# A linear attention block with a squared-ReLU MLP: w_in's products of four slices in pairs by seven block products

## The chip, the cores and the metric

One core of a Trainium2 chip runs the whole program. The metric is device time in microseconds, from the first to the last instruction; the number for a kernel is the median over its runs.

## The reference

Linear attention with a decay per head, in blocks along the sequence (4 batches, 8 heads, 768 positions, 64 features a head), and then an MLP over the 3072 tokens:

```
intra = ((q_block @ k_block.T) * decay_mask) @ v_block
inter = (q_block * lam**(pos+1)) @ kv_state
out   = intra + inter
kv_state = lam**block * kv_state + (k_block * lam**(block-1-pos)).T @ v_block

x = out, laid out as (3072, 512)
h = x @ w_in            # w_in  (512, 2048)
g = max(h, 0)**2
result = g @ w_out      # w_out (2048, 512)
```

All inputs and the result are float32.

## The kernel before

Tokens are taken in tiles of C = 128, NT = 24 of them (six to a batch), t counting them; G = 4 tiles make a slice of N = 512 tokens, and there are NM = 6 slices, m = 0 to 5 (in the text, slice 1 is m = 0). The 2048 hidden features are NF = 16 blocks of 128, f counting them.

A float32 product is made of three products of reduced float32 (F32R): each operand is split into a high part and the rest, and high x high, rest x high and high x rest are added. The weights lie split in SBUF for the whole program, `wh` and `wl`, w_in's block f in place `w_in(f)` and w_out's in `w_out(f)`; the loading, rounding and splitting of the weights is spread over slice 1.

One step (m, f) is `hidden(m, f)`, twelve matmuls of 512 columns into a PSUM bank `h` (4 pieces of the 512 inner features x 3 parts), then on ScalarE `square(h)` (ReLU, square rounded to `gh`, square), on VectorE `rest` (the difference `gl`), and `project`, twelve matmuls of 512 columns that add to the slice's four output banks `acc`. `project` of a step stands in the next step, behind the next `hidden`, so that ScalarE and VectorE have twelve matmuls of time. After f = 15 the four banks are copied out and stored.

The attention of a slice is made during the slice before it: in the steps f of slice m tile t = 4(m+1) + f // 4 is taken, in four parts by f % 4: `prep_k` and, behind the projection, `scores` (part 0), `prep_q` and `masked` (1), `attend` (2: the update of the state, the products within the block and with the state, and `split`, which makes `xh` and `xl` of the result), `decay` (3). So half a tile's matmuls at most stand between two products of w_in. `attend` is followed by the loads of tile t + 2 (`load_qk`, `load_kv`), into two buffers taken in turn. `prep_q`, `prep_k` and `decay` run on GpSimd, all transfers are issued by SP.

The order on every engine is the order in which the code is written; nothing reorders it. Waits are semaphores between the engines, put in where data or buffers need them. PSUM has four `acc` banks, two `h` banks and two for attention (`ps_a`: first the two score banks, then the banks of the output o and of the state update u).

Of the kernel before, what the change touches and what calls it, by code (L numbers as in the profile page):

```python
# [19 lines left out]
NCB = S // C  # L20
NT = B * NCB
DM = H * D
DF = 2048
KT = DM // P
NF = DF // P
G = 4
N = G * C
NM = NT // G

NLOT = NF + 1


@with_exitstack
def body(ctx: ExitStack, tc: tile.TileContext, qT, kT, kvq, lam, w, out):
    nc = tc.nc
    const = ctx.enter_context(tc.tile_pool(name="const", bufs=1))
    io = ctx.enter_context(tc.tile_pool(name="io", bufs=2))
    wk = ctx.enter_context(tc.tile_pool(name="wk", bufs=2))  # L40
    small = ctx.enter_context(tc.tile_pool(name="small", bufs=1))
    ps_acc = ctx.enter_context(tc.tile_pool(name="ps_acc", bufs=G, space=PSUM))
    ps_h = ctx.enter_context(tc.tile_pool(name="ps_h", bufs=2, space=PSUM))
    ps_a = ctx.enter_context(tc.tile_pool(name="ps_a", bufs=2, space=PSUM))
    V = nc.vector
# [12 lines left out]
    kv = const.tile([P, NPR, P], F32, name="kv")  # L58
# [9 lines left out]


    feat, tok, lent = {}, {}, {}  # L70

    def load_qk(t):
        if t in (2, 3):
            lent[t] = wk.tile([P, 2, KT * C, 2], F32, name=f"lent{t}", tag=("xh", "xl")[t - 2])
            x = lent[t][:, 0].rearrange("p a b -> p (a b)")
        else:
            x = io.tile([P, 2 * DM], F32, name="qk_sb")
        feat[t] = x.rearrange("p (k a b) -> p k a b", k=2, a=NPR)
        for k, y in enumerate((kT, qT)):
            nc.sync.dma_start(out=feat[t][:, k], in_=y[t])  # L80

    def load_kv(t):
        if t in (2, 3):
            x = lent[t][:, 1].rearrange("p a b -> p (a b)")
        else:
            x = io.tile([P, 2 * DM], F32, name="kv_sb")
        nc.sync.dma_start(out=x, in_=kvq[t, :, 0 : 2 * DM])
        x = x.rearrange("p (k h d) -> p k h d", k=2, h=H)
        tok[t] = x[:, 0], x[:, 1]


    wh = const.tile([P, 2 * NF, DM], F32R, name="wh")
    wl = const.tile([P, 2 * NF, DM], F32R, name="wl")

    def w_in(f):
        return 2 * f - 1 if f else 0

    def w_out(f):
        return 2 * f + 2 if f < NF - 1 else 2 * NF - 1
# [29 lines left out]
    def first(u):  # L129
        first_hi(u)  # L130
        first_lo(u)
# [167 lines left out]
    def scores(t, pool, name):  # L299
        sc_of[t] = [pool.tile([P, DM], F32, name=name) for _ in range(2)]  # L300
        k_, q_ = feat[t][:, 0], feat[t][:, 1]
        for p in range(NPR):
            for j, r in enumerate(rows):
                nc.tensor.matmul(  # L304
                    sc_of[t][j][:, p * C : (p + 1) * C], k_[r, p], q_[r, p],
                    start=True, stop=True, skip_group_check=True,
                )

    def prep_q(t):
        if t % NCB:  # L310
            nc.gpsimd.tensor_tensor(out=feat[t][:, 1], in0=feat[t][:, 1], in1=qpow, op=ALU.mult)  # L311

    def prep_k(t):
        if t % NCB < NCB - 1:
            x = tok[t][0].rearrange("p (a j) d -> p a j d", j=2)
            y = near.rearrange("p j a c -> p a j c")[:, :, :, T - 1 : T]
            nc.gpsimd.tensor_tensor(out=x, in0=x, in1=y.broadcast_to([P, NPR, 2, D]), op=ALU.mult)

    def masked(t):
        a_of[t] = []  # L320
        for j in range(2):
            a = wk.tile([P, NPR, C], F32, name="a", tag="gl" if t in (1, 3) else "a")
            V.tensor_tensor(  # L323
                out=a, in0=sc_of[t][j].rearrange("p (a b) -> p a b", a=NPR),
                in1=mask[:, j], op=ALU.mult,
            )
            a_of[t].append(a)
# [38 lines left out]
    def split(t, o):  # L366
        xh, xl = xs_of[t // G]
        cs = slice(t % G * C, (t % G + 1) * C)
        o = o.rearrange("p (a b) -> p a b", a=KT)
        nc.scalar.copy(xh[:, :, cs], o)  # L370
        return lambda: V.tensor_tensor(
            out=xl[:, :, cs], in0=o, in1=xh[:, :, cs].bitcast(F32), op=ALU.subtract
        )

    def attend(t):

        o = ps_a.tile([P, DM], F32, name="att")
        u = ps_a.tile([P, DM], F32, name="att")
        news(t, u)
        within(t, o, True, not t % NCB)  # L380
        before(t, o, False, True)
        update(t, u)
        split(t, o)()

    def decay(t):
        if t % NCB < NCB - 2:
            for j, r in enumerate(rows):
                nc.gpsimd.tensor_tensor(  # L388
                    out=kvd[r], in0=kv[r, :, rows[j]],
                    in1=qpow[r, :, C - 1 : C].broadcast_to([D, NPR, D]), op=ALU.mult,  # L390
                )


    g_of, accs, stage = {}, {}, []

    def hidden(m, f, xh, xl):
        h = ps_h.tile([P, N], F32, name="h")
# [9 lines left out]
    def square(h):  # L407
        nc.scalar.activation(h, h, AF.Relu)  # L408
        gh = wk.tile([P, N], F32R, name="gh")
        nc.scalar.activation(gh, h, AF.Square)  # L410
        nc.scalar.activation(h, h, AF.Square)  # L411
        return gh

    def rest(m, f, r, gh):
        gl = wk.tile([P, N], F32R, name="gl")
        V.tensor_tensor(out=gl, in0=r, in1=gh.bitcast(F32), op=ALU.subtract)  # L416
        g_of[m, f] = gh, gl

    def project(m, f):
        gh, gl = g_of.pop((m, f))  # L420
        if f == 0:
            accs[m] = [ps_acc.tile([P, DM], F32, name="acc") for _ in range(G)]
        end = f == NF - 1
        j = w_out(f)

        def high(i):
            cs = slice(i * C, (i + 1) * C)
            nc.tensor.matmul(accs[m][i], gh[:, cs], wh[:, j], start=f == 0, stop=False)  # L428
            nc.tensor.matmul(accs[m][i], gh[:, cs], wl[:, j], start=False, stop=False)  # L429

        def low(i):
            cs = slice(i * C, (i + 1) * C)
            nc.tensor.matmul(accs[m][i], gl[:, cs], wh[:, j], start=False, stop=end)  # L433
            if end:
                if i == 0:
                    stage.append(wk.tile([P, G, DM], F32, name="o", tag="raw"))
                o = stage[-1][:, i]
                if i % 2:
                    V.tensor_copy(o, accs[m][i])
                else:  # L440
                    nc.scalar.copy(o, accs[m][i])
                t = m * G + i
                nc.sync.dma_start(out=out[t * C : (t + 1) * C, :], in_=o)

        n = 2 if end and m == NM - 1 else 1
        for i in range(0, G, n):
            for step in (high, low):
                for k in range(i, i + n):
                    step(k)

    def new_x(m):
        xs_of[m] = [wk.tile([P, KT, N], F32R, name=n, tag=n) for n in ("xh", "xl")]
# [75 lines left out]
    wload(3)  # L528

    prev = None  # L530
    for m in range(NM):
        if m + 1 < NM:
            new_x(m + 1)
        for f in range(NF):
            t = (m + 1) * G + f // 4
            step = f % 4 if t < NT else None
            h = hidden(m, f, *xs_of[m])
            if m == 0:

                u_ = f + 2  # L540
                if u_ < NLOT:
                    for op in (clamp, shift, sign):
                        op(u_)
                if f == 0:
                    news(3, u[3])
                    update(3, u[3])
                    decay(3)
                    gh = square(h)
                    rest(m, f, h, gh)
                if f:  # L550
                    upper(u_ - 1)
                    lower(u_ - 1)
                    turn(u_ - 1)
                if u_ < NLOT:
                    rounded(u_)
                    wload(u_ + 2)
            if step == 0:
                prep_k(t)
            if step == 1:
                prep_q(t)  # L560
            if step == 3:
                decay(t)
            if m or f:
                gh = square(h)
                rest(m, f, h, gh)
            if step == 1:
                masked(t)
            if step == 2:
                attend(t)
                if t + 2 < NT:  # L570
                    load_qk(t + 2)
                    load_kv(t + 2)
            if m == 0 and u_ + 1 < NLOT:
                first(u_ + 1)
            if prev is not None:
                project(*prev)
            prev = (m, f)
            if step == 0:
                scores(t, ps_a, "att")
    project(*prev)  # L580


def _limit():
# [50 lines left out]
```

## Time and profile before

| | |
|---|---|
| median of 3 runs | 636.17 us (635.25 to 638.42) |
| profiled execution, first to last instruction | 636.4 us; the page has no other time of that execution |
| TensorE busy | 624.6 us, 98% |
| VectorE, ScalarE, GpSimd busy | 222.1, 233.9, 88.5 us |
| moved by the transfer engines | 48.81 MB in 18488 packets |

A page's row of an engine gives busy time, share of the span and instructions. PE is TensorE, PEld its weight loads (beside the matmuls), DVE VectorE, ACT ScalarE, POOL GpSimd, SP the engine that issues transfers. A group's row gives line, engine, operation, output <- inputs, shapes, count, then busy time and mean ns of one, and the idle time ahead of it with who ended it. In a timeline, a row has start and length in us; the matmuls in a row overlap, and their rate is read from start to start.

### The profile page before, as it was taken

Reading aid. Unit: us, or ns where it says so; the run is one execution under the profiler, and the core shown is the slowest. Engines: PE = TensorE matmul, PEld = TensorE weight load, DVE = VectorE, ACT = ScalarE, POOL = GpSimd, SP = SyncE. Lnnn points to the kernel's source line nnn. Section 1 sums busy time; section 2 is a strip of 40 time slices with the busy share of each in tenths; the row PEclk is TensorE's granted clock in tenths of the full one; section 3 lists DMA queues with packets and bytes.
Section 4 is the critical chain, followed back from the end, with each engine's and each line's share of the span. In section 5 each row is a group of like instructions: output and inputs, shape, how many; then the busy total and the mean of one; then the engine's idle time right before and its main releaser. Section 6 shows DMA issues by size and latency. Waiting matters only on the chain.

```text
span 636.4 us, 8960 instructions
## 1 busy us (share of the span) xinstructions
PE 624.6 (98%) x3744; PEld 508.8 (80%) x3744; DVE 222.1 (35%) x341; ACT 233.9 (37%) x383; POOL 88.5 (14%) x105
## 2 busy tenths in 40 slices
PE   8889999999999999999999999999999999999997
PEld 5768888888788888888888888888888888888885
DVE  6899999922222023121221221212312212211111
ACT  3277777723232324232323232323232323322232
POOL 4631222321010100210120010101201000000000
PEclk9799999999999999999999999999999999999999
DMA  8647576232021013010211202102302000100001
GB/s 310 253 134 239 161 261 205 96 131 67 1 66 52 17 67 106 27 67 2 67 57 76 67 1 76 58 1 67 122 11 67 1 2 0 67 1 1 0 1 66
DMA packets 18488, 48.81 MB, mean 77 GB/s; under 512 B 2064, under 2 KB 2064, under 8 KB 18448
## 3 DMA queue, kind: packets, MB, share of 16 engines
q1 hardware_dynamic: 18448, 48.24, 22.3%
q8 instruction: 29, 0.48, 0.3%
q14 instruction: 11, 0.09, 0.0%
HBM read 41.94 MB, written 6.29 MB: 76 GB/s over the span
## 4 chain that ended last, share of the span: by engine, by line
PE 95%; DVE 2%; DMA 1%; POOL 0%; issue 0%; ACT 0%; SPq 0%; DVEq 0%; POOLq 0%
PE h L401 40%; PE acc L428 14%; PE acc L429 14%; PE acc L433 14%; PE att L304 3%; PE att L343 3%; PE att L350 2%; PE att L335 2%; PE att L65 1%; DMA raw<-in_w 1%; DVE mask L288 1%; PE acc L304 0%; DVE A L152 0%; PE h L304 0%; PE h L248 0%
## 5 line engine op out<-in xcount | busy, mean ns | idle before, releaser
L416 DVE TENSOR_TENSOR gl<-h,gh 128x512 fp32r<-128x512 f32 x96 | 66.3, 691 | 395.8 <-ACT h L411 395.8
L408 ACT ACTIVATE h<-h 128x512 f32<-128x512 f32 x96 | 55.9, 582 | 346.8 <-PE h L401 346.7
L428 PE MATMUL acc<-wh,gh 128*128 128x512 f32 x384 | 151.7, 395 | 0.0
L429 PE MATMUL acc<-wl,gh 128*128 128x512 f32 x384 | 149.6, 390 | 0.0
L433 PE MATMUL acc<-wh,gl 128*128 128x512 f32 x384 | 149.0, 389 | 0.0
L401 PE MATMUL h<-xh,wh 128*128 128x512 f32 x384 | 105.3, 396 | 0.7 <-ACT xh L370 0.7
L401 PE MATMUL h<-xh,wl 128*128 128x512 f32 x384 | 103.0, 390 | 2.0 <-DVE wl L161 2.0
L401 PE MATMUL h<-xl,wh 128*128 128x512 f32 x384 | 102.6, 389 | 0.0
L428 PEld LDWEIGHTS acc<-wh,gh 128*128 128x128 f32 x384 | 72.1, 188 | 17.9 <-issue 2.1
L401 PEld LDWEIGHTS h<-xh,wl 128*128 128x128 f32 x384 | 72.0, 188 | 17.7 <-DVE wl L161 2.4
L433 PEld LDWEIGHTS acc<-wh,gl 128*128 128x128 f32 x384 | 72.1, 188 | 15.2
L401 PEld LDWEIGHTS h<-xl,wh 128*128 128x128 f32 x384 | 72.1, 188 | 15.0
L401 PEld LDWEIGHTS h<-xh,wh 128*128 128x128 f32 x384 | 70.5, 188 | 16.9 <-ACT xh L370 0.9
L429 PEld LDWEIGHTS acc<-wl,gh 128*128 128x128 f32 x384 | 72.1, 188 | 14.2
L410 ACT ACTIVATE gh<-h 128x512 fp32r<-128x512 f32 x96 | 57.6, 600 | 3.0
L411 ACT ACTIVATE h<-h 128x512 f32<-128x512 f32 x96 | 57.0, 594 | 0.0
L311 POOL TENSOR_TENSOR qk_sb<-qk_sb,qpow 128x512 f32<-128x512 f32 x18 | 23.3, 1295 | 200.9 <-PE att L304 200.9
L388 POOL TENSOR_TENSOR kvd<-kv,qpow 64x256 f32<-64x256 f32 x32 | 21.4, 668 | 155.9 <-DVE kv L360 86.6
L343 PE MATMUL att<-a,kv_sb 128*64 128x128 f32 x336 | 23.6, 282 | 2.5 <-DVE a L323 2.5
L323 DVE TENSOR_TENSOR a<-att,mask 128x512 f32<-128x512 f32 x40 | 25.6, 681 | 0.0
L122 ACT ACTIVATE A<-raw 128x1024 f32<-128x1024 f32 (+1 forms) x17 | 18.6, 1095 | 18.8 <-DMA raw<-in_w 15.5
L304 PEld LDWEIGHTS att<-qk_sb 64*128 64x128 f32 x320 | 19.4, 187 | 6.8 <-issue 6.7
(91 smaller groups left out, 385.3 us busy)
## 6 DMA issues: line engine op xcount, KB each, us to landing
raw<-in_w SPq DMA_DIRECT2D x32, 512.0 KB, 4.6
kv_sb<-in_kvq SPq DMA_DIRECT2D x22, 512.0 KB, 4.7
out_x<-o SPq DMA_DIRECT2D x24, 256.0 KB, 2.2
qk_sb<-in_kT SPq DMA_DIRECT2D x22, 256.0 KB, 2.6
qk_sb<-in_qT SPq DMA_DIRECT2D x22, 256.0 KB, 3.0
lent<-in_kvq SPq DMA_DIRECT2D x2, 512.0 KB, 7.6
lent<-in_kT SPq DMA_DIRECT2D x2, 256.0 KB, 7.9
lent<-in_qT SPq DMA_DIRECT2D x2, 256.0 KB, 7.3
```

What stands on the lines that cost most here:

```text
L304: nc.tensor.matmul(sc_of[t][j][:, p * C : (p + 1) * C], k_[r, p], q_[r, p], start=True, stop=True, skip_group_check=True,)
L311: nc.gpsimd.tensor_tensor(out=feat[t][:, 1], in0=feat[t][:, 1], in1=qpow, op=ALU.mult)
L323: V.tensor_tensor(out=a, in0=sc_of[t][j].rearrange("p (a b) -> p a b", a=NPR), in1=mask[:, j], op=ALU.mult,)
L343: nc.tensor.matmul(o[r, p * C : (p + 1) * C], tok[t][1][:, 2 * p + j, :], a[j][:, p, :], start=first and p == 0, stop=last, skip_group_che ...
L401: nc.tensor.matmul(h, wt[:, w_in(f), kt * P : (kt + 1) * P], x[:, kt], start=k == 0, stop=k == 11)
L408: nc.scalar.activation(h, h, AF.Relu)
L410: nc.scalar.activation(gh, h, AF.Square)
L411: nc.scalar.activation(h, h, AF.Square)
L416: V.tensor_tensor(out=gl, in0=r, in1=gh.bitcast(F32), op=ALU.subtract)
L428: nc.tensor.matmul(accs[m][i], gh[:, cs], wh[:, j], start=f == 0, stop=False)
L429: nc.tensor.matmul(accs[m][i], gh[:, cs], wl[:, j], start=False, stop=False)
L433: nc.tensor.matmul(accs[m][i], gl[:, cs], wh[:, j], start=False, stop=end)
```

## The change

Slices 1 and 2 keep their products. Slices 3 and 4 make one duo (d = 0), slices 5 and 6 another (d = 1). Within a duo, blocks f1 = 2i and f2 = 2i + 1 of w_in make a pair: w_in's two blocks and the two halves of the inner 512 features give a 2 x 2 block matrix, x of the two slices and the two halves another one. The four result blocks (f1, f2) x (m1, m2) are made from seven block products (`product`, six matmuls each) instead of eight; the sums that this needs are taken of blocks of w_in (`w_sums`, once), of blocks of x (`x_sums`, in place in `held`) and of results (in `pair`).

- w_in's seven factors of a pair, split into two parts each, are written to device memory (`wd`) in slice 2 (`w_parts`, six transfers), and fetched again for every product of both duos (`fetch`, 256 KB each) into a ring of eight places.
- The attention of slices 3 and 4 (tiles 8 to 15) is made in steps 0 to 8 of slice 2, a tile a step; that of slices 5 and 6 (tiles 16 to 23) in the eight pairs of the first duo, a tile a pair. `attend` copies its result to `held` unsplit. From tile 17 on the loads have one buffer.
- x's seven factors, split, lie in the places of `wh` and `wl` that w_in's blocks 1 to 14 had (`x_parts`), made in steps 9 to 15 of slice 2, and for the second duo in steps 1 to 7 of slice 4.
- The results of the second slice of a duo are kept squared in SBUF (`r_of`, `kept`), and its steps are only a copy and a difference (`again`) and `project`.

```diff
+PLAIN = 2
+SOLO = 17
+NPAIR = NF // 2
+RING = 8
+HALF = DM // 2
...
-    io = ctx.enter_context(tc.tile_pool(name="io", bufs=2))
+    dram = ctx.enter_context(tc.tile_pool(name="dram", bufs=1, space=bass.MemoryType.DRAM))
...
+    io = {(n, i): const.tile([P, 2 * DM], F32, name=f"{n}{i}") for n in ("qk", "kv") for i in range(2)}
+    def home(t):
+        return t % 2 if t < SOLO else 0
...
-        split(t, o)()
+        if t < PLAIN * G:
+            split(t, o)()
+        else:
+            cs = slice(t % G * C, (t % G + 1) * C)
+            nc.scalar.copy(held[t // G % 2][:, :, cs], o.rearrange("p (a b) -> p a b", a=KT))
...
+    W11, W12, WS1, WS2, WS3, WS4, W22 = range(7)
+    X11, X21, X22, XT1, XT3, XT2, XT4 = range(7)
+    FACTORS = (
+        (W11, X11), (WS2, XT2), (W12, X21), (WS3, XT3), (WS1, XT1), (W22, XT4), (WS4, X22),
+    )
+    wd = dram.tile([NPAIR, P, 7, 2, HALF], F32, name="wd")
+    held = []
+    def w_sums(i):
+        p1, p2 = w_in(2 * i), w_in(2 * i + 1)
+        F = wk.tile([P, 2, DM], F32, name="F", tag="A")
+        for k, p in enumerate((p1, p2)):
+            V.tensor_tensor(out=F[:, k], in0=wh[:, p].bitcast(F32), in1=wl[:, p].bitcast(F32), op=ALU.add)
+        a11, a12, a21, a22 = (F[:, k, b * HALF : (b + 1) * HALF] for k in range(2) for b in range(2))
+        S = wk.tile([P, 4, HALF], F32, name="S", tag="A")
+        add(S[:, 0], a21, a22)
+        sub(S[:, 1], S[:, 0], a11)
+        sub(S[:, 2], a11, a21)
+        sub(S[:, 3], a12, S[:, 1])
+        return S
+    def w_parts(i, S):
+        p1, p2 = w_in(2 * i), w_in(2 * i + 1)
+        hl = wk.tile([P, 2, 4, HALF], F32R, name="hl", tag="raw")
+        nc.scalar.copy(hl[:, 0], S)
+        V.tensor_tensor(out=hl[:, 1], in0=S, in1=hl[:, 0].bitcast(F32), op=ALU.subtract)
+        for k, x in enumerate((wh, wl)):
+            x = x.bitcast(F32)
+            nc.sync.dma_start(
+                out=wd[i, :, W11 : W12 + 1, k], in_=x[:, p1].rearrange("p (b n) -> p b n", b=2)
+            )
+            nc.sync.dma_start(out=wd[i, :, W22, k], in_=x[:, p2, HALF:DM])
+            nc.sync.dma_start(out=wd[i, :, WS1 : WS4 + 1, k], in_=hl[:, k].bitcast(F32))
+    def x_slot(j, k):
+        return (wh, wl)[k][:, w_in(j + 1)]
+    def x_sums(c):
+        (b11, b21), (b12, b22) = (
+            (x[:, 0:2], x[:, 2:4]) for x in held
+        )
+        if c == XT1:
+            sub(b11, b12, b11)
+        if c == XT3:
+            sub(b12, b22, b12)
+        if c == XT2:
+            sub(b22, b22, b11)
+        if c == XT4:
+            sub(b21, b21, b22)
+    def x_parts(c):
+        (b11, b21), (b12, b22) = (
+            (x[:, 0:2], x[:, 2:4]) for x in held
+        )
+        x = {X11: b11, X21: b21, X22: b22, XT1: b11, XT3: b12, XT2: b22, XT4: b21}[c]
+        for kt in range(2):
+            hi, lo = (x_slot(2 * c + kt, k) for k in range(2))
+            nc.scalar.copy(hi, x[:, kt])
+            V.tensor_tensor(out=lo, in0=x[:, kt], in1=hi.bitcast(F32), op=ALU.subtract)
+    ring = {}
+    def place_of(n):
+        k = n % RING
+        if k < 4:
+            return (wh, wl)[k % 2][:, w_in(0 if k < 2 else NF - 1)]
+        if "tile" not in ring:
+            ring["tile"] = wk.tile([P, 4, DM], F32R, name="ring", tag="xh")
+        return ring["tile"][:, k - 4]
+    def fetch(n):
+        if n < (NM - PLAIN) // 2 * NPAIR * 7:
+            i, k = n // 7 % NPAIR, FACTORS[n % 7][0]
+            nc.sync.dma_start(
+                out=place_of(n).bitcast(F32), in_=wd[i, :, k].rearrange("p k n -> p (k n)")
+            )
+    def product(n, bank, first):
+        w, c = place_of(n), FACTORS[n % 7][1]
+        q = 0
+        for kw, kx in ((0, 0), (1, 0), (0, 1)):
+            for kt in range(2):
+                nc.tensor.matmul(
+                    bank, w[:, kw * HALF + kt * P : kw * HALF + (kt + 1) * P], x_slot(2 * c + kt, kx),
+                    start=first and q == 0, stop=q == 5, skip_group_check=True,
+                )
+                q += 1
+        fetch(n + RING)
+    def squared(m, f, h):
+        rest(m, f, h, square(h))
+    r_of = []
+    def later(f):
+        if f >= len(r_of):
+            if f < 4:
+                x = wk.tile([P, 2, DM], F32, name="r", tag="A")
+                r_of.extend(x[:, k] for k in range(2))
+            elif f < 8:
+                x = io["qk" if f < 6 else "kv", 1]
+                r_of.extend(x[:, k * DM : (k + 1) * DM] for k in range(2))
+            else:
+                x = wk.tile([P, G, DM], F32, name="r", tag="raw")
+                r_of.extend(x[:, k] for k in range(G))
+        return r_of[f]
+    def kept(r):
+        nc.scalar.activation(r, r, AF.Relu)
+        nc.scalar.activation(r, r, AF.Square)
+    def again(m, f):
+        gh = wk.tile([P, N], F32R, name="gh")
+        nc.scalar.copy(gh, r_of[f])
+        rest(m, f, r_of[f], gh)
+    def pair(d, i, temp, between, attention):
+        m1 = PLAIN + 2 * d
+        n = (d * NPAIR + i) * 7
+        f1, f2 = 2 * i, 2 * i + 1
+        p1, u2, u3, c21 = (temp[:, k] for k in range(4))
+        later(f2)
+        X = ps_h.tile([P, N], F32, name="h")
+        product(n, X, True)
+        nc.scalar.copy(p1, X)
+        Y = ps_h.tile([P, N], F32, name="h")
+        product(n + 1, Y, True)
+        add(u2, Y, p1)
+        product(n + 2, X, False)
+        attention(0)
+        product(n + 3, Y, False)
+        squared(m1, f1, X)
+        add(u3, Y, p1)
+        attention(1)
+        between()
+        Z = ps_h.tile([P, N], F32, name="h")
+        product(n + 4, Z, True)
+        add(r_of[f2], Z, u3)
+        product(n + 5, Y, False)
+        add(c21, Y, p1)
+        product(n + 6, Z, False)
+        add(r_of[f1], Z, u2)
+        squared(m1, f2, c21)
+        for f in (f2, f1):
+            kept(r_of[f])
+        attention(2)
+        project(m1, f1)
...
-    for m in range(NM):
-        if m + 1 < NM:
-            new_x(m + 1)
+    for m in range(PLAIN):
+        if m == 0:
+            new_x(1)
+        else:
+            held += [
+                wk.tile([P, KT, N], F32, name=f"held{k}", tag=n) for k, n in enumerate(("xh", "xl"))
+            ]
         for f in range(NF):
-            t = (m + 1) * G + f // 4
-            step = f % 4 if t < NT else None
             h = hidden(m, f, *xs_of[m])
             if m == 0:
-
+                t = G + f // 4
+                step = f % 4
                 u_ = f + 2
                 if u_ < NLOT:
                     for op in (clamp, shift, sign):
@@ -554,30 +722,98 @@
                 if u_ < NLOT:
                     rounded(u_)
                     wload(u_ + 2)
-            if step == 0:
-                prep_k(t)
-            if step == 1:
-                prep_q(t)
-            if step == 3:
-                decay(t)
-            if m or f:
-                gh = square(h)
-                rest(m, f, h, gh)
-            if step == 1:
-                masked(t)
-            if step == 2:
-                attend(t)
-                if t + 2 < NT:
+                if step == 0:
+                    prep_k(t)
+                if step == 1:
+                    prep_q(t)
+                if step == 3:
+                    decay(t)
+                if f:
+                    gh = square(h)
+                    rest(m, f, h, gh)
+                if step == 1:
+                    masked(t)
+                if step == 2:
+                    attend(t)
                     load_qk(t + 2)
                     load_kv(t + 2)
-            if m == 0 and u_ + 1 < NLOT:
-                first(u_ + 1)
-            if prev is not None:
+                if u_ + 1 < NLOT:
+                    first(u_ + 1)
+                if prev is not None:
+                    project(*prev)
+                if step == 0:
+                    scores(t, ps_a, "att")
+            else:
+                t = 2 * G + f
+                if f < 2 * G:
+                    prep_k(t)
+                if 1 <= f <= 2 * G:
+                    masked(t - 1)
+                    S = w_sums(f - 1)
+                squared(m, f, h)
+                if 1 <= f <= 2 * G:
+                    w_parts(f - 1, S)
+                    attend(t - 1)
+                    if t + 1 < SOLO:
+                        load_qk(t + 1)
+                        load_kv(t + 1)
+                    decay(t - 1)
+                if f == 2 * G + 1:
+                    fetch(0)
+                    fetch(1)
+                if f > 2 * G:
+                    x_sums(f - 2 * G - 1)
+                    x_parts(f - 2 * G - 1)
                 project(*prev)
+                if f < 2 * G:
+                    scores(t, ps_a, "att")
+                    prep_q(t)
             prev = (m, f)
-            if step == 0:
-                scores(t, ps_a, "att")
-    project(*prev)
+    temp = wk.tile([P, 4, DM], F32, name="temp", tag="xl")
+    for n in range(2, RING):
+        fetch(n)
+    for d in range((NM - PLAIN) // 2):
+        m1, m2 = PLAIN + 2 * d, PLAIN + 2 * d + 1
+        last = d == (NM - PLAIN) // 2 - 1
+        for i in range(NPAIR):
+            t = (PLAIN + 2) * G + i
+            def attention(step):
+                if last:
+                    return
+                if step == 0:
+                    scores(t, ps_a, "att")
+                    prep_k(t)
+                    prep_q(t)
+                if step == 1:
+                    masked(t)
+                if step == 2:
+                    attend(t)
+                    decay(t)
+                    if i + 1 < NPAIR:
+                        load_qk(t + 1)
+                        load_kv(t + 1)
+            p = prev
+            if p[0] == m2 - 2 and p[1] == NF - 1 and d:
+                places = [r_of[k] for k in range(G)]
+            else:
+                places = None
+            pair(d, i, temp, lambda: project(*p, place=places), attention)
+            prev = (m1, 2 * i + 1)
+        again(m2, 0)
+        project(*prev, place=[temp[:, k] for k in range(G)])
+        for f in range(NF):
+            if f + 1 < NF:
+                again(m2, f + 1)
+            if not last and 1 <= f <= 7:
+                x_sums(f - 1)
+                x_parts(f - 1)
+            if f + 1 < NF:
+                project(m2, f)
+        prev = (m2, NF - 1)
+    project(*prev, place=[r_of[k] for k in range(G)])
 def _limit():
```

On TensorE, before, the products of w_in in one step of slice 4, the attention of a tile and the start of the projection of the step before (h is the bank, xh and xl are x's parts, wh and wl w_in's):

```order
L401 MATMUL h_2441<-xh_1295,wh_89 128x512 x4
L401 MATMUL h_2441<-xh_1295,wl_90 128x512 x4
L401 MATMUL h_2441<-xl_1296,wh_89 128x512 x4
L335 MATMUL att_2461<-kv_sb_2139 64x64 x8
L343 MATMUL att_2460<-a_2425,kv_sb_2139 64x128
```

Now, in a pair of the first duo, the first three products (banks 2506 and 2515) and the start of the tile's scores; both operands lie in wh, wl or the ring:

```order
L550 MATMUL h_2506<-wh_92,ring_2340 128x512 x4
L550 MATMUL h_2506<-wl_93,ring_2340 128x512 x2
L550 MATMUL h_2515<-wh_92 128x512 x4
L550 MATMUL h_2515<-wl_93,wh_92 128x512 x2
L550 MATMUL h_2506<-wh_92,wl_93 128x512 x4
L550 MATMUL h_2506<-wl_93 128x512 x2
L313 MATMUL att_2531<-qk0_88 128x128
```

and, behind a projection, the last three (banks 2572, 2515, 2572), ahead of the rest of the tile's attention:

```order
L550 MATMUL h_2572<-wh_92,wl_93 128x512 x4
L550 MATMUL h_2572<-wl_93 128x512 x2
L550 MATMUL h_2515<-wh_92,ring_2340 128x512 x4
L550 MATMUL h_2515<-wl_93,ring_2340 128x512 x2
L550 MATMUL h_2572<-wh_92,ring_2340 128x512 x4
L550 MATMUL h_2572<-wl_93,ring_2340 128x512 x2
L352 MATMUL att_2607<-a_2556,kv0_90 64x128
```

Twelve matmuls a block have become six a product, and a bank is gone back to after one other product.

On SP in slice 2, before, the loads of two tiles (eight steps of f):

```order
L80 DMA qk_sb_1437<-in_kT 128x512
L80 DMA qk_sb_1437<-in_qT 128x512
L87 DMA kv_sb_1440<-in_kvq 128x1024
L80 DMA qk_sb_1614<-in_kT 128x512
L80 DMA qk_sb_1614<-in_qT 128x512
L87 DMA kv_sb_1617<-in_kvq 128x1024
```

Now, one step of f (hl is the split block sums):

```order
L496 DMA wd_180<-wh_92 128x2x256
L499 DMA wd_180<-wh_92 128x256
L500 DMA wd_180<-hl_1471 128x4x256
L496 DMA wd_180<-wl_93 128x2x256
L499 DMA wd_180<-wl_93 128x256
L500 DMA wd_180<-hl_1471 128x4x256
L89 DMA qk1_89<-in_kT 128x512
L89 DMA qk1_89<-in_qT 128x512
L96 DMA kv1_91<-in_kvq 128x1024
```

The loads of a tile now stand behind six stores, and come four times as often.

On VectorE in slice 4, before, three steps with a tile's masks, state and split:

```order
L416 TENSOR_TENSOR gl_3299<-h_3281,gh_3296 128x512
L323 TENSOR_TENSOR a_3301<-att_3271,mask_143 128x512
L323 TENSOR_TENSOR a_3303<-att_3272,mask_143 128x512
L416 TENSOR_TENSOR gl_3334<-h_3317,gh_3331 128x512
L360 TENSOR_TENSOR kv_82<-kvd_180,att_3337 64x4x64 x2
L371 TENSOR_TENSOR xl_2718<-att_3336,xh_2717 128x4x128
L416 TENSOR_TENSOR gl_3402<-h_3383,gh_3399 128x512
```

Now, steps 4 to 6 of slice 4, the second slice of the first duo (wl and held: x's parts and sums for the second duo):

```order
L429 TENSOR_TENSOR gl_3610<-qk1_89,gh_3608 128x512
L218 TENSOR_TENSOR held0_1283<-held1_1284,held0_1283 128x1024
L526 TENSOR_TENSOR wl_93<-held0_1283,wh_92 128x512 x2
L429 TENSOR_TENSOR gl_3631<-kv1_91,gh_3629 128x512
L218 TENSOR_TENSOR held1_1284<-held1_1284 128x1024
L526 TENSOR_TENSOR wl_93<-held1_1284,wh_92 128x512 x2
L429 TENSOR_TENSOR gl_3652<-kv1_91,gh_3650 128x512
```

The differences gl, for which the projections wait, have sums and splits of x between them.

More of the change, by code (lines that the diff above doesn't have):

```diff
@@ L76, in load_qk @@
         else:
-            x = io.tile([P, 2 * DM], F32, name="qk_sb")
+            x = io["qk", home(t)]
         feat[t] = x.rearrange("p (k a b) -> p k a b", k=2, a=NPR)
@@ L85, in load_kv @@
         else:
-            x = io.tile([P, 2 * DM], F32, name="kv_sb")
+            x = io["kv", home(t)]
         nc.sync.dma_start(out=x, in_=kvq[t, :, 0 : 2 * DM])
@@ L391, in decay @@
                 )
-    g_of, accs, stage = {}, {}, []
+    g_of, accs = {}, {}
     def hidden(m, f, xh, xl):
@@ L417, in rest, with project @@
         g_of[m, f] = gh, gl
-    def project(m, f):
+    def project(m, f, place=None):
         gh, gl = g_of.pop((m, f))
@@ L424, in project @@
         j = w_out(f)
+        if end and place is None:
+            x = wk.tile([P, G, DM], F32, name="o", tag="raw")
+            place = [x[:, i] for i in range(G)]
         def high(i):
@@ L434, in low @@
             if end:
-                if i == 0:
-                    stage.append(wk.tile([P, G, DM], F32, name="o", tag="raw"))
-                o = stage[-1][:, i]
+                o = place[i]
                 if i % 2:
```

## The prediction

> **What bounds the kernel now.** I read the page's busy times first, then its chain of work that ended last.
>
> ```profile
> span 636.4 us, 8960 instructions
> ...
> PE 624.6 (98%) x3744; PEld 508.8 (80%) x3744; DVE 222.1 (35%) x341; ACT 233.9 (37%) x383; POOL 88.5 (14%) x105
> ...
> PEclk9799999999999999999999999999999999999999
> ...
> PE 95%; DVE 2%; DMA 1%; POOL 0%; issue 0%; ACT 0%; SPq 0%; DVEq 0%; POOLq 0%
> ```
>
> TensorE is busy 98% of the span and makes 95% of the chain, at full granted clock from the third of the page's 40 stretches on. So matmuls set the time, and a matmul less is time less as long as nobody makes TensorE wait instead. The profiled execution (span 636.4) lies 0.2 us above the median of the runs, 636.17; I work against 636.4. The timeline of TensorE, two stretches of slices 2 and 3, gives the price of its work:
>
> ```profile
> 199.64 1.07 PE L401 MATMUL h<-xl,wh 128*128 128x512 f32 x4
> ...
> 200.63 0.69 PE L335 MATMUL att<-kv_sb 128*64 128x64 f32 x16
> ...
> 203.00 0.50 PE L428 MATMUL acc<-wh,gh 128*128 128x512 f32 x1
> ```
>
> ```profile
> 255.84 1.07 PE L401 MATMUL h<-xh,wh 128*128 128x512 f32 x4
> 256.75 1.07 PE L401 MATMUL h<-xh,wl 128*128 128x512 f32 x4
> 257.66 1.07 PE L401 MATMUL h<-xl,wh 128*128 128x512 f32 x4
> 258.56 0.39 PE L428 MATMUL acc<-wh,gh 128*128 128x512 f32 x1
> ...
> 266.50 0.39 PE L433 MATMUL acc<-wh,gl 128*128 128x512 f32 x1
> 266.81 1.16 PE L304 MATMUL att<-qk_sb 64*128 64x128 f32 x16
> 267.91 1.19 PE L401 MATMUL h<-xh,wh 128*128 128x512 f32 x4
> ```
>
> From 255.84 to 258.56 twelve matmuls of 512 columns start: 2.72 us, or 0.2267 us each, and the step from one bank to the next (257.66 to 258.56, four matmuls, 0.90) costs nothing extra. A matmul's end is shown 0.39 us after its start, so 0.16 us after the next has begun. Scores of one tile take 267.91 - 266.73 = 1.2 us (266.73 is the L433 start and 0.227), the rest of a tile's attention 203.00 - 200.55 = 2.45 us.
>
> **Part 1: the matmuls that go.** A pair of f and a pair of slices needed 4 x 12 = 48 matmuls of w_in; seven products of six are 42. With 8 f pairs and 2 slice pairs that is 96 fewer, 96 x 0.2267 = 21.8 us, all on TensorE's path. Nothing else of TensorE's work changes in number: projections and attention keep theirs. The Trainium skill (TensorE: Matmul & The Clock Gate, Back-to-back issue gap) gives 215.7 ns for such a matmul when warm, by which the saving would be estimated at 20.7 us; the same place names 131 ns as sustained, by which it would be 12.6 us. The row's 227 ns decides, and it agrees with the first within 5% and not with the second.
>
> **Part 2: slice 2 becomes dense.** Tiles 8 to 15 are now done there, one a step, in steps f = 1 to 8, with the block sums of w_in between. The prices:
>
> ```profile
> L323 DVE TENSOR_TENSOR a<-att,mask 128x512 f32<-128x512 f32 x40 | 25.6, 681 | 0.0
> L416 DVE TENSOR_TENSOR gl<-h,gh 128x512 fp32r<-128x512 f32 x96 | 66.3, 691 | 395.8 <-ACT h L411 395.8
> L161 DVE TENSOR_TENSOR wl<-A,wh 128x1024 fp32r<-128x1024 f32 x15 | 18.3, 1219 | 0.5 <-ACT wh L158 0.5
> L360 DVE TENSOR_TENSOR kv<-kvd,att 64x256 f32<-64x256 f32 x28 | 11.7, 418 | 0.7 <-PE att L350 0.3
> L408 ACT ACTIVATE h<-h 128x512 f32<-128x512 f32 x96 | 55.9, 582 | 346.8 <-PE h L401 346.7
> L410 ACT ACTIVATE gh<-h 128x512 fp32r<-128x512 f32 x96 | 57.6, 600 | 3.0
> L411 ACT ACTIVATE h<-h 128x512 f32<-128x512 f32 x96 | 57.0, 594 | 0.0
> L158 ACT CAST wh<-A 128x1024 fp32r<-128x1024 f32 x15 | 15.7, 1045 | 1.2 <-DVE A L152 1.2
> L158 ACT CAST wh<-A 128x512 fp32r<-128x512 f32 x2 | 1.2, 620 | 0.0
> L317 POOL TENSOR_TENSOR kv_sb<-kv_sb,near 128x512 f32<-128x512 f32 x18 | 20.2, 1122 | 5.3 <-DMA kv_sb<-in_kvq 4.3
> L311 POOL TENSOR_TENSOR qk_sb<-qk_sb,qpow 128x512 f32<-128x512 f32 x18 | 23.3, 1295 | 200.9 <-PE att L304 200.9
> L388 POOL TENSOR_TENSOR kvd<-kv,qpow 64x256 f32<-64x256 f32 x32 | 21.4, 668 | 155.9 <-DVE kv L360 86.6
> ```
>
> A step of TensorE is 2.72 + 2.72 + 1.2 + 2.45 = 9.1 us. VectorE needs in it, in order: masks 2 x 0.68, two whole-block sums 2 x 0.69, four sums of 256 columns at about 0.42 (the 256-column row is L360), gl 0.69, hl 1.22, the state 2 x 0.42: 7.2 us. ScalarE: squares 1.8, hl 1.05, copy 0.6: 3.4. GpSimd: 1.12 + 1.30 + 2 x 0.67 = 3.8. All fit; the tight place is the bank of u. Counted from the step's start, ScalarE's squares end at 2.72 + 0.16 + 1.8 = 4.7, its hl copy at 5.75, VectorE's hl at 7.0 and the state update behind it, which frees u, at 7.8. The next scores take that bank at 2.72 + 2.45 + 2.72 = 7.9. So 0 to 0.3 us can show in each of 8 steps; I take 1 us in all, with 0 and 2.4 as ends.
>
> The queue of SP gets nine transfers a step where slice 2 had three every four. Each step writes 7 blocks x 2 halves x 128 rows = 1792 runs of 1 KB (1.84 MB) and reads one tile's 1 MB. No 1 KB run is in the trace. Nearest are two windows' last columns (DMA share, GB/s): the first holds only stores of 2 KB rows, the second loads of 2 and 4 KB rows.
>
> ```profile
> 540.00:550.00 10.00, 10.00 (x46) 8.29 (x45) 2.58 (x4) 3.66 (x7) 0.00 (x0) 1.00 0.20 77
> ...
> 204.00:208.00 4.00, 4.00 (x19) 3.30 (x18) 0.73 (x2) 0.00 (x0) 0.00 (x0) 1.00 0.79 256
> ```
>
> 77 / 0.20 is 385 GB/s at full share, 24 GB/s an engine, 85 ns for 2 KB; 256 / 0.79 is 324. If time goes with bytes, a 1 KB run takes 42 ns and the writes 1792 x 42 / 16 = 4.8 us; if it goes by the run, 85 ns and 9.5 us. With 1.05 MB at 324 GB/s, 3.2 us, a step needs 8.0 or 12.7 us of the transfer engines. I take bytes, since the 4 KB rows are no cheaper a byte than the 2 KB rows; then it hides under the 9.1.
>
> **Part 3: the pairs.** I call the products P1 to P7 in order; each is 6 x 0.2267 = 1.36 us. With the two projections a pair is 66 matmuls, 15.0 us without attention. Every add of the pair (0.69) and copy (0.6) has other matmuls beside it: P3 goes on in P1's bank after the copy of P1, with P2's 1.36 as cover against 0.16 + 0.6; P7 goes on in P5's bank after an add, with P6 as cover against 0.16 + 0.69, 0.5 us to spare. The new bank of P5 needs squares and gl of the first result (0.16 + 1.8 + 0.69 = 2.7), covered by P4 and a projection, 4.1. ScalarE's queue is longest behind P6: add 0.69, then seven operations of 0.6, so free 5.1 us after P6; the next copy wants it at P7 + projection + P1 + 0.16 = 5.6. All at nothing; if one cover failed it would cost 16 times its lack. VectorE holds 7 x 0.69 = 4.8 (7.0 with a tile's masks and state), ScalarE 11 x 0.6 = 6.6.
>
> Tiles 16 to 23 ride in the first eight pairs with one buffer instead of two: the load of the next tile waits for this tile's attention. From there TensorE has a projection, P1, P2 and P3, 2.72 + 4.08 = 6.8 us, before the next scores. Landing times:
>
> ```profile
> out_x<-o SPq DMA_DIRECT2D x24, 256.0 KB, 2.2
> qk_sb<-in_kT SPq DMA_DIRECT2D x22, 256.0 KB, 2.6
> qk_sb<-in_qT SPq DMA_DIRECT2D x22, 256.0 KB, 3.0
> ```
>
> 2.6 to 3.0 us for q and k: hidden. The weight fetches (7 a pair, 256 KB, asked for eight products ahead, over 12 us) are hidden likewise.
>
> **Part 4: the second slice of a duo.** Each f is only its projection, 2.72 us, against a copy of 0.6 and gl of 0.69. In the first duo, four of the f also carry a sum of 1024 columns and two splits. Their chain crosses engines: copy 0.62, gl 0.69, sum 1.22, two copies 0.62: 3.8 us a step, 1.05 over the projection, 4.2 in four steps. gl is ready 1.3 after a projection's start and wanted at 2.72 + 0.45: 1.9 slack. Charge 2 (0 if the copies overlap better, 4.2 without the slack).
>
> **Part 5: seams.** The last x split of slice 2 stands ahead of the first copy of P1 on ScalarE: gl ends 2.7 after the last hidden, sum 1.2, two copies 1.2: 5.1, copy 5.7; P3 wants it at 2 x 2.72 = 5.4: 0.3. In the second duo's first pair a result buffer is still being stored: about 0.2 by the 2.2 us row. Start and end of the program do not change.
>
> **Sum.** 636.4 - 21.8 + 1 + 2 + 0.3 + 0.2 = 618.1, so 618. With the ends of these terms 615 to 621.
>
> **Rivals.**
> (a) The 1 KB writes bind slice 2. By the run (85 ns) a step takes 12.7 instead of 9.1, in seven steps with a load 25 us: 643, slower. It begins at (9.1 - 3.2) x 16 / 1792 = 53 ns a run and makes the kernel slower by over 0.5% from 80 ns. For it: reads and writes mix, and nothing like it is in the trace. Against it: bytes price both rows above. At 64 ns it would be 627. Chance 0.14, a third of it beyond 633.
> (b) The head of a product costs TensorE a gap, since it waits on a fetch and on another engine. The switch to attention does cost one: 200.63 stands 0.08 behind, and 266.81 as much, with weights loaded late. If each of 112 heads cost the 0.35 us that the weight loads sit idle there (row below), 39 us: 657. It is slower by over 0.5% from 21.6 / 112 = 0.19 us. Against it: the hand-over at 258.56, which also waits for other engines, costs nothing. Chance 0.08, half of it mild (0.1 us, 629).
>
> ```profile
> 200.63 0.55 PEld L335 LDWEIGHTS att<-kv_sb 128*64 128x64 f32 x16 [0.35 <-issue]
> ```
>
> (c) Fetches run one behind another. 7 x 2.6 = 18.2 us a pair against 15.0, in eight pairs 26 us: 644. Against it: three loads are issued 0.4 us apart and land within 3 to 5 us, so they overlap:
>
> ```profile
> 203.17 0.33 SPq L80 DMA_DIRECT2D qk_sb<-in_kT  x1
> 203.54 0.43 SPq L80 DMA_DIRECT2D qk_sb<-in_qT  x1
> 204.02 0.43 SPq L87 DMA_DIRECT2D kv_sb<-in_kvq  x1
> ```
>
> Chance 0.04. The Trainium skill (DMA: Bandwidth & Descriptors, Measured) speaks for it: it puts about 2.0 us of fixed cost on a transfer and asks for 1 MiB at a time; by its fit 256 KB takes an estimated 2.6 us, as the row says, and whether such transfers overlap is what these issue rows answer.
>
> **Numbers.** 0.5% is 3.2 us, about what a measurement of this kernel can tell. The sum's own case has 0.72 (613 to 622); something unseen that saves more, 0.02. Faster: 0.74, two thirds of (a), half of (b): 0.87. Slower: (c), the rest of (b), a few hundredths of (a), together 0.09. The same: 0.04. Range 613 to 632: up to there it holds the first case, (a) to some 70 ns and a mild (b).
>
> **What would show it.** Matmuls of 512 columns fall by 96 and keep 0.227 us from start to start within a pair; TensorE stays at 97% or above. Right for part 2: steps 1 to 8 of slice 2 take 9.1 to 9.4 us and the transfer share there is about 0.9. Wrong: steps of 10 us or more with TensorE behind loads or ScalarE (a); idle time ahead of product heads (b), or ahead of them with a transfer as releaser (c); over 4 us of waits for gl in the first duo's second slice (part 4).

## The result, and the profile after

| | before | after |
|---|---|---|
| median of four runs each | 635.72 us | 616.87 us |
| fastest to slowest run | 635.25 to 638.42 | 615.28 to 617.79 |
| ratio of after to before, 95% interval | | 0.9695 (0.9668 to 0.9722) |
| profiled execution: its time / its span | 638.42 / 636.4 us | 617.79 / 616.0 us |

The kernel is 18.9 us faster, 3.0%; the forecast was 618 with 613 to 632. The profiled execution's time is 1.8 to 2.0 us more than its span, and in both kernels the profiled execution was the slowest of the four.

The page of the kernel after: span, engines, the transfer engines' row of the 40 stretches, and the chain by engine and by line (L550 is the products, L414 the plain products of w_in, L444 to L449 the projections).

```profile
span 616.0 us, 9349 instructions
...
PE 605.4 (98%) x3648; PEld 490.5 (80%) x3648; DVE 325.7 (53%) x497; ACT 271.6 (44%) x435; POOL 90.2 (15%) x105
...
DMA  8747485417999900665554554310064444430101
...
PE 95%; DVE 3%; DMA 1%; issue 0%; POOL 0%; ACT 0%; DVEq 0%; SPq 0%; POOLq 0%
PE h L550 25%; PE acc L444 15%; PE acc L449 14%; PE acc L445 14%; PE h L414 14%; PE att L352 3%; PE att L313 3%; PE att L359 3%; PE att L344 2%; PE att L70 1%; DMA raw<-in_w 1%; DVE mask L297 1%; DVE A L161 0%; DVE A L155 0%; PE acc L313 0%
```

TensorE has 96 matmuls less and is busy for as large a share as before; VectorE went from 222 to 326 us, ScalarE from 234 to 272, and the chain hardly noticed. The transfer engines' row has a new plateau of nines, in slice 2.

TensorE's timeline in a pair of the first duo, products P1 to P3, the scores of a tile, P4 and the head of the projection:

```profile
269.56 1.07 PE L550 MATMUL h<-wh,ring 128*128 128x512 f32 x4
...
270.92 1.07 PE L550 MATMUL h<-wh 128*128 128x512 f32 x4
...
272.28 1.07 PE L550 MATMUL h<-wh,wl 128*128 128x512 f32 x4
273.18 0.61 PE L550 MATMUL h<-wl 128*128 128x512 f32 x2
273.73 1.16 PE L313 MATMUL att<-qk 64*128 64x128 f32 x16
274.82 1.19 PE L550 MATMUL h<-wh 128*128 128x512 f32 x4
275.85 0.63 PE L550 MATMUL h<-wl,wh 128*128 128x512 f32 x2
276.32 0.39 PE L444 MATMUL acc<-wh,gh 128*128 128x512 f32 x1
```

269.56 to 270.92 to 272.28 is 1.36 us a product, six times 0.227: a product's head costs nothing, though it waits for a fetch and for another engine. P4 behind the scores takes 1.50: attention charges 0.1 on the way in and 0.1 on the way out, as it did before.

Steps of slice 2 (busy time of the engines, then TensorE's clock, transfer share, GB/s):

```profile
149.08:158.43 9.35, 9.35 (x91) 7.52 (x89) 6.78 (x12) 3.11 (x5) 4.38 (x4) 1.00 1.00 329
158.43:167.77 9.34, 9.34 (x90) 7.51 (x88) 6.77 (x12) 3.11 (x5) 1.30 (x1) 1.00 0.93 308
...
194.93:204.28 9.35, 9.35 (x91) 7.52 (x89) 6.78 (x12) 3.11 (x5) 4.26 (x5) 1.00 1.01 328
```

TensorE is busy in all of a step's 9.35 us and waits for nobody, beside transfer engines that are busy 93 to 100% of it. All of it hides. A share near 1.00 is not yet the most that these engines move: they move 308 to 329 GB/s in these rows, and 383 to 389 in the run with doubled stores below.

Slice 4 is where TensorE does wait. Its timeline around three projections (idle time and its releaser in brackets):

```profile
421.80 0.39 PE L445 MATMUL acc<-wl,gh 128*128 128x512 f32 x1
422.23 0.50 PE L449 MATMUL acc<-wh,gl 128*128 128x512 f32 x1
...
424.40 0.39 PE L449 MATMUL acc<-wh,gl 128*128 128x512 f32 x1
425.06 0.50 PE L444 MATMUL acc<-wh,gh 128*128 128x512 f32 x1 [0.27 <-ACT gh L581]
425.39 0.40 PE L445 MATMUL acc<-wl,gh 128*128 128x512 f32 x1
425.95 0.50 PE L449 MATMUL acc<-wh,gl 128*128 128x512 f32 x1 [0.16 <-DVE gl L429]
```

Starts are 0.43, 0.66 and 0.56 us apart where 0.227 is due, and the matmul behind a wait takes 0.335. Summed by starts over the slice, five such waits (two for gh, three for gl) cost 2.27 us. The brackets add up to 0.87 in the view of waits, since idle time is counted there only from the end of the last matmul, 0.16 us after the next was due, and the slow restart of 0.11 is not idle at all.

### The profile page after: what moved, and what is told of

It is laid out like the page before. It is cut to its first block, busy times and chain, and to the rows that moved or that the text cites. A ratio compares the mean times of both kernels' runs of the same rounds, so it can differ in the third digit from the quotient of the medians.

```text
span 616.0 us, 9349 instructions
## 1 busy us (share of the span) xinstructions
PE 605.4 (98%) x3648; PEld 490.5 (80%) x3648; DVE 325.7 (53%) x497; ACT 271.6 (44%) x435; POOL 90.2 (15%) x105
## 4 chain that ended last, share of the span: by engine, by line
PE 95%; DVE 3%; DMA 1%; issue 0%; POOL 0%; ACT 0%; DVEq 0%; SPq 0%; POOLq 0%
PE h L550 25%; PE acc L444 15%; PE acc L449 14%; PE acc L445 14%; PE h L414 14%; PE att L352 3%; PE att L313 3%; PE att L359 3%; PE att L344 2%; PE att L70 1%; DMA raw<-in_w 1%; DVE mask L297 1%; DVE A L161 0%; DVE A L155 0%; PE acc L313 0%
## 5 line engine op out<-in xcount | busy, mean ns | idle before, releaser
L444 PE MATMUL acc<-wh,gh 128*128 128x512 f32 x384 | 152.0, 396 | 0.6 <-ACT gh L581 0.6
L449 PE MATMUL acc<-wh,gl 128*128 128x512 f32 x384 | 149.4, 390 | 0.4 <-DVE gl L429 0.3
L444 PEld LDWEIGHTS acc<-wh,gh 128*128 128x128 f32 x384 | 72.1, 188 | 19.2 <-issue 2.9
L449 PEld LDWEIGHTS acc<-wh,gl 128*128 128x128 f32 x384 | 72.1, 188 | 16.7 <-DVE gl L429 1.6
L421 ACT ACTIVATE h<-h 128x512 f32<-128x512 f32 x48 | 27.9, 582 | 116.4 <-PE h L414 82.6
L218 DVE TENSOR_TENSOR temp<-h,temp 128x512 f32<-128x512 f32 x48 | 33.1, 690 | 74.9 <-PE h L550 46.4
L429 DVE TENSOR_TENSOR gl<-h,gh 128x512 fp32r<-128x512 f32 x48 | 33.1, 689 | 71.3 <-ACT h L424 71.3
L550 PE MATMUL h<-wh,ring 128*128 128x512 f32 x224 | 60.5, 392 | 0.0
L550 PEld LDWEIGHTS h<-wh,ring 128*128 128x128 f32 x224 | 41.7, 188 | 9.2 <-DVE r L218 0.4
L320 POOL TENSOR_TENSOR qk<-qk,qpow 128x512 f32<-128x512 f32 x18 | 23.4, 1299 | 106.1 <-PE att L313 104.5
L414 PE MATMUL h<-xh,wh 128*128 128x512 f32 x128 | 35.9, 402 | 0.7 <-ACT xh L379 0.7
L414 PE MATMUL h<-xh,wl 128*128 128x512 f32 x128 | 34.5, 391 | 2.0 <-DVE wl L170 2.0
L414 PE MATMUL h<-xl,wh 128*128 128x512 f32 x128 | 34.6, 393 | 0.0
L550 PE MATMUL h<-wl,ring 128*128 128x512 f32 x112 | 34.5, 389 | 0.0
```

The costliest lines, as they stand in the source:

```text
L218: lambda o, x, y, op=op: V.tensor_tensor(out=o, in0=x, in1=y, op=op)
L414: nc.tensor.matmul(h, wt[:, w_in(f), kt * P : (kt + 1) * P], x[:, kt], start=k == 0, stop=k == 11)
L550: nc.tensor.matmul(bank, w[:, kw * HALF + kt * P : kw * HALF + (kt + 1) * P], x_slot(2 * c + kt, kx), start=first and q == 0, stop=q == 5, ...
```

## The experiments

All were timed against the kernel before on the same chip, in two groups: the doubled stores and the shorter fetches beside a kernel before of 636.28 us, the others beside one of 635.77. First the changed kernel again, as the ruler.

> The changed kernel again, as the ruler for the others: 616.9 us, ratio 0.970 to the kernel before.

616.65 us, ratio 0.9706 (0.9683 to 0.9729).

The profiles give a second measure: the time from the first matmul of slice 2, up to which all kernels run the same code, to the end of the span. It is 502.1 us before, and 482.9 and 482.8 in two executions of the changed kernel. Below, "from slice 2 on" means this time.

**Eight products again.**

```diff
...
-        product(n + 6, Z, False)
+        product(n + 6, Z, False, times=2)
```

> The seventh product of every pair is made twice over into its bank (six more matmuls of 512 columns, so the sums differ there): eight products a pair, 96 more matmuls, all other work of the change kept. If time goes by the count of matmuls: 616.9 + 96 x 0.227 = 638.7, that is 2.5 above the kernel before, which is then all that the sums, splits, stores and fetches cost. If the gain came from elsewhere (a better cover of attention, say), well below that: 617 to 630.

638.44 us, ratio 1.0036 (1.0018 to 1.0055): 21.8 above the ruler, the price of 96 matmuls. That the medians agree with it to the tenth is luck, since the runs of this kernel alone lie between 636.46 and 640.29; from slice 2 on it is 504.5 us, 21.7 above the ruler. It is 2.7 above its kernel before (635.77; 1.1 to 3.5 by the interval) and 2.4 above it from slice 2 on. So the gain is the matmuls', and all the rest of the change, with its 100 us of VectorE, costs some 2.5 us.

**The cover of P7 taken away.**

```diff
-    (W11, X11), (WS2, XT2), (W12, X21), (WS3, XT3), (WS1, XT1), (W22, XT4), (WS4, X22),
+    (W11, X11), (WS2, XT2), (W12, X21), (WS3, XT3), (WS1, XT1), (WS4, X22), (W22, XT4),
...
-        product(n + 5, Y, False)
-        add(c21, Y, p1)
-        product(n + 6, Z, False)
-        add(r_of[f1], Z, u2)
+        product(n + 5, Z, False)
+        add(r_of[f1], Z, u2)
+        product(n + 6, Y, False)
+        add(c21, Y, p1)
```

> Products 6 and 7 change places, so that the product which goes on in the fifth's bank follows it at once, behind VectorE's add. Theory (an add of 0.69 and 0.16 behind the product's end is covered by the product between): the cover is gone, 0.9 us in 16 pairs, and ScalarE's queue moves 1.36 us back, 0.2 us in eight pairs: 616.9 + 16 = 633. Rival (these hand-overs were never near the limit): 617.

639.56 us, ratio 1.0049 (1.0029 to 1.0070): 22.9 above the ruler where 16 was expected. The whole gain is gone by the order of two products. TensorE's timeline, the fifth product and the one behind it:

```profile
479.58 1.07 PE L550 MATMUL h<-wh,wl 128*128 128x512 f32 x4
480.49 0.61 PE L550 MATMUL h<-wl 128*128 128x512 f32 x2
481.88 1.21 PE L550 MATMUL h<-wh,ring 128*128 128x512 f32 x4 [0.78 <-DVE r L218]
482.93 0.62 PE L550 MATMUL h<-wl,ring 128*128 128x512 f32 x2
```

And its waits, for that add, 16 of them (the result r lies in places named r, kv and qk), and for ScalarE's copy (us in total, times, longest):

```profile
PE h L550 <- DVE r L218: 9.9, 12, 1.3
...
PE h L550 <- DVE kv L218: 1.6, 2, 0.8
PE h L550 <- DVE qk L218: 1.6, 2, 0.8
...
PE h L550 <- ACT temp L592: 1.3, 7, 0.2
```

From 480.49 to 481.88 is 1.39 where two matmuls are 0.45: 0.94 lost, about as expected, but 481.88 to 482.93 is 1.05 for four matmuls instead of 0.91, the slow restart. That is 1.08 a pair and 17.3 in 16 pairs. ScalarE's copy, expected 0.2 late in eight pairs, costs 0.45 (0.18 idle, 0.16 ahead of it, 0.11 of restart) in the seven where it is late, 3.2 more; in the first pair of the second duo the wait is 0.5 longer; and two late starts in the projections of slice 6 cost 0.9. That is 21.9 of the 22.3 that the kernel takes longer from slice 2 on (505.1 us). The mechanism was right, the price of a wait was too low.

**The splits of x spread out in slice 4.**

```diff
-            if not last and 1 <= f <= 7:
-                x_sums(f - 1)
-                x_parts(f - 1)
+            if not last and f % 2 and f <= 13:
+                x_sums(f // 2)
+                x_parts(f // 2)
```

> The seven splits of x for the second duo stand in steps 1, 3, ... 13 of slice 4 instead of 1 to 7. Theory (the chain of copies, sums and differences of two steps outruns the projections): the waits of TensorE for gh and gl in slice 4 (0.87 us in the profile) go, 615.8 to 616.0, at the edge of what the runs tell, but plain in the profile. Rival (they come from the copy of gh alone): the waits stay.

613.48 us, ratio 0.9650 (0.9623 to 0.9678); this interval lies below the ruler's: the best kernel of the study, 22.3 below the kernel before. TensorE's timeline at the same place:

```profile
428.20 0.39 PE L445 MATMUL acc<-wl,gh 128*128 128x512 f32 x1
428.43 0.39 PE L449 MATMUL acc<-wh,gl 128*128 128x512 f32 x1
428.66 0.39 PE L444 MATMUL acc<-wh,gh 128*128 128x512 f32 x1
428.88 0.39 PE L445 MATMUL acc<-wl,gh 128*128 128x512 f32 x1
```

No start in slice 4 is late any more. From the last product of the first duo to the first of the second the profile has 48.6 us instead of 50.9: 2.3 us, where 0.9 to 1.1 was expected, because I had taken the loss from the view of waits and not from the starts. From slice 2 on it is 480.5 us against 482.8, the same 2.3. The medians differ by 3.2; the rest is within what they vary.

**The stores of slice 2 made twice.**

```diff
+    wd2 = dram.tile([NPAIR, P, 7, 2, HALF], F32, name="wd2")
...
-            nc.sync.dma_start(out=wd[i, ...
+            for y in (wd, wd2):
+                nc.sync.dma_start(out=y[i, ...
```

> All stores of w_in's factors in slice 2 are made twice, the second time to a tensor that nobody reads: 3584 runs of 1 KB a step. Theory (transfer engines were 90 to 100% busy in steps 1 to 8 and hid with nothing to spare): a step needs 3584 x 46 ns / 16 = 10.3 us and 2.6 for the loads, 12.9 against 9.35, so 20 to 27 us more: 637 to 644. Rival (stores wait for nobody and drain later): 617 to 620.

636.39 us, ratio 0.9999 (0.9981 to 1.0017): 19.5 above the 616.9 of the changed kernel, just under the range expected. Two windows of slice 2 (columns as above):

```profile
160.00:170.00 10.00, 7.96 (x71) 6.00 (x69) 8.59 (x12) 3.20 (x5) 4.42 (x4) 1.00 1.09 383
170.00:180.00 10.00, 7.26 (x58) 5.97 (x60) 4.04 (x8) 1.50 (x3) 1.28 (x1) 0.83 1.08 389
```

And two of TensorE's waits, the longest in total and another one of slice 2:

```profile
PE att L313 <- DMA qk<-in_qT: 12.1, 5, 3.5
...
PE att L359 <- POOL qk L320: 1.6, 1, 1.6
```

The engines that move data are full, and what comes late is the load of q and k, which stands behind twelve stores on SP; scores, and with them all of TensorE's queue, wait for it. These two rows make 13.7 of the 18.9 us that the kernel takes longer from slice 2 on (501.7 us). Most of the rest is the clock: behind three of the waits it was halved for 3.4 us (last section), and half the work of that time is an estimated 1.7 us each. At 389 GB/s for a share of 1.08, an engine moves 22.5 GB/s, so a run of 1 KB takes 45 ns: by bytes, as taken. The packets of 1 KB in the trace have a median of 46 ns. In the changed kernel the same loads, behind half as many stores, come in time.

**Fetches four and two products ahead.**

```diff
-RING = 8
+RING = 4      # and 2
```

> Weights of the products are fetched four products ahead instead of eight. A fetch lands 2.8 us after its issue, four products are 5.4 us: theory (hidden with room) 617. Rival (fetches run one behind another, 7 x 2.8 = 19.6 a pair against 15): it was hidden only by the eight in flight, 630 or more.

> Fetched two products ahead. A product wants its weights 1.36 us after the fetch is issued where no projection lies between (third and seventh of a pair), and 4.1 where one does. Theory (2.8 us to landing, overlapped): 1.5 us late twice a pair, 16 pairs: 48 us, 665. Rival (fetches one behind another): 16 x 4.6 and more, 690.

Four: 617.17 us, ratio 0.9693 (0.9675 to 0.9711), as the changed kernel. Two: 675.08 us, ratio 1.0597 (1.0567 to 1.0627), 58 above it where 48 was expected. So fetches overlap; four places are enough and two are not (three were not tried). With two, TensorE waits for the weights:

```profile
PE h L550 <- DMA wh<-wd: 24.2, 16, 1.7
PE h L550 <- DMA wl<-wd: 23.6, 17, 1.5
```

33 waits, two a pair as expected and a short one, 1.45 us each by this view, which again leaves out the 0.16 and the restart, 0.08 here. With both they come to 56 of the 57.3 us that the kernel takes longer from slice 2 on (540.1 us).

## Why the prediction was right

**Part 1** (21.8 us) is shown by the experiment with an eighth product: 638.44 - 616.65 = 21.8, and 21.7 from slice 2 on. The 12.6 us by the second figure of the Trainium skill (TensorE: Matmul & The Clock Gate, Back-to-back issue gap) is refuted by both measures. The medians could not tell 20.7 from 21.8; the rows can, with 0.2267 us from start to start.

**Part 2** took 1 us for the bank of u. It cost nothing: no wait of TensorE stands in steps 1 to 8. The step is 9.35 us and not 9.1 because my price of attention left out the slower first matmul behind each of its two parts (0.11 twice), which the kernel before pays as well. The transfers were taken by bytes, 8.0 us a step; measured is a share of 0.93 to 1.00 of 9.35. The writes are not the reason: a packet of 1 KB took 46 ns here too. The packets of the loads were slower, 102 and 231 ns in the mean for 2 and 4 KB against medians of 84 and 159; why is not shown. The price of rival (a), 85 ns a run, is refuted by the 46 ns. That the transfer engines can bind slice 2 is real all the same: with twice the bytes to store it cost 19.5 us. In the changed kernel there was more room than the share tells, for a step's 2.88 MB are 7.4 us at the 389 GB/s of that run.

**Part 3**, every hand-over at nothing: confirmed, and by the experiment without cover shown to rest on the order of P6 and P7. The sentence that a failed cover costs its lack 16 times is too low; it costs the lack (0.16 + 0.69), 0.09 more until the next matmul starts, and 0.11 for the restart.

**Part 4** took 2 us for slice 4 and measured 2.3; the chain's 3.8 us a step is 3.72 in the trace, by the starts of gl:

```profile
421.49 0.68 DVE L429 TENSOR_TENSOR gl<-kv,gh 128x512 fp32r<-128x512 f32 x1
...
425.21 0.68 DVE L429 TENSOR_TENSOR gl<-r,gh 128x512 fp32r<-128x512 f32 x1
```

Spreading the splits removed it, so it is shown and not only argued. **Part 5**: the first seam cost 0.14 us of the 0.3. The second cost the 0.2 that was forecast, in this execution. In the first pair of the second duo VectorE's add waits for the store, and P7, which waits for the add, starts 0.09 late and has the 0.11 of restart (a row of VectorE's timeline, then two of TensorE's):

```profile
455.88 0.69 DVE L218 TENSOR_TENSOR r<-h,temp 128x512 f32<-128x512 f32 x1 [1.18 <-DMA out_x<-r]
...
456.08 0.61 PE L550 MATMUL h<-wl,ring 128*128 128x512 f32 x2
456.63 1.21 PE L550 MATMUL h<-wh,ring 128*128 128x512 f32 x4
```

In the ruler's profile P7 starts on time there.

**The sum.** The first matmul of slice 2 in the timeline of TensorE, before:

```profile
134.29 1.07 PE L401 MATMUL h<-xh,wh 128*128 128x512 f32 x4
```

and after:

```profile
133.11 1.07 PE L414 MATMUL h<-xh,wh 128*128 128x512 f32 x4
```

From there to the end it is (636.4 - 134.3) - (616.0 - 133.1) = 19.2 us less; 21.8 less 2.3, 0.14 and 0.2 is 19.2. The other 1.2 us of the two spans lie ahead of slice 2, where the code does the same work, and are no work of the change: the eight profiled executions of the changed kernel and its variants reach that row anywhere between 131.2 and 133.9 us. One step of the working was wrong and did no harm: I set the span, 636.4, against the runs' median, 636.17. The time that belongs to that span is 638.42, and the sum made from it is 620.1, 3.2 too high; made from the median it is 617.9. The costs were taken at 3.5 us and measured 2.6, nearly all of it in slice 4.

Rivals (b) and (c) are refuted: heads cost nothing, and four fetches in flight are enough. What the prediction cites for (c) from the Trainium skill (DMA: Bandwidth & Descriptors) as 2.0 us of fixed cost stands in the section Anatomy of one DMA, for transfers that GpSimd issues; these are issued by SP.

## What to carry to other kernels

When one engine is busy 98% of the time, fewer of its instructions is the gain, and the count times the row's start-to-start time is its size, even if the others get half as much work again. What has to be looked after is then each hand-over: the longest chain of other engines between two instructions that share a bank or a buffer, against what stands between them in the queue; the order of two products was worth the whole gain here, and work for later that is put between the links of such a chain (the splits of x) belongs in every second step rather than in every one. Price a wait by the starts of the waiting engine's instructions, not by the idle time that a view names.

## What the runs showed of the hardware

A TensorE matmul of 512 columns that starts behind a wait for another engine, or behind attention's small matmuls, takes about 0.335 us to the next start instead of 0.227 from slice 2 on: 0.11 us of restart. Behind the waits for fetches, in the kernel that fetches two products ahead, it takes 0.306, so 0.08.

Waits cost the clock as well. TensorE's timeline in the kernel with doubled stores:

```profile
172.74 1.16 PE L313 MATMUL att<-qk 64*128 64x128 f32 x16 [3.17 <-DMA qk<-in_qT]
173.83 2.03 PE L414 MATMUL h<-xh,wh 128*128 128x512 f32 x4
...
221.34 1.78 PE L313 MATMUL att<-qk 64*128 64x128 f32 x16 [2.52 <-DMA qk<-in_qT]
```

and windows of it, the clock being the third column from the end:

```profile
180.00:190.00 10.00, 8.43 (x75) 6.52 (x72) 5.81 (x10) 2.56 (x5) 1.06 (x1) 1.00 1.08 391
190.00:200.00 10.00, 6.51 (x42) 4.92 (x39) 4.61 (x8) 2.16 (x4) 1.77 (x3) 0.89 1.08 390
...
220.00:230.00 10.00, 8.66 (x79) 7.21 (x80) 6.42 (x10) 2.92 (x5) 3.88 (x4) 0.83 1.07 382
```

Behind waits of 3.17, 3.49 and 2.52 us the granted clock is halved for 3.4 us (0.83 in the window from 170, 0.89 from 190, 0.83 from 220), and four matmuls take 2.03 us instead of 1.07. Behind a wait of 1.6 us it stays (1.00 from 180), as behind all the waits of up to 1.7 us for fetches in the kernel that fetches two products ahead. In between it goes both ways. In slice 1 every kernel waits some 2 us for the same part of w_in. After it, in the changed kernel (timeline and a window behind it):

```profile
43.14 1.19 PE L414 MATMUL h<-xh,wl 128*128 128x512 f32 x4 [1.97 <-DVE wl L170]
...
45.00:48.00 3.00, 3.00 (x34) 2.42 (x34) 2.93 (x5) 2.97 (x5) 0.51 (x1) 0.50 0.89 261
```

and in the kernel before:

```profile
45.47 1.20 PE L401 MATMUL h<-xh,wl 128*128 128x512 f32 x4 [1.96 <-DVE wl L161]
...
47.00:50.00 3.00, 2.72 (x49) 2.33 (x49) 2.93 (x6) 2.97 (x5) 0.84 (x1) 1.00 0.79 221
```

Six of the eight profiles of the changed kernel and its variants have this drop, two and the kernel before do not; what decides is not shown. From the first product of w_in to the first of slice 2 it is 103.2 to 103.6 us with the drop and 102.1 without.

The Trainium skill (TensorE: Matmul & The Clock Gate, Why this matters for your kernels) asks for no gaps above about 3 us, since the clock then goes back to half. These traces agree above 3 us, but show the drop behind 2.52 us too, and at times behind 2; here the measurement decides.
